# An attention and Fourier-mixing kernel on one core: x is kept on the chip between the two stages

## The chip, the cores and the metric

The kernel runs on one core of one Trainium2 chip. The metric is device microseconds of one execution, from the start of the program to its end. The engines of the core work from queues of their own, each in program order: TensorE (PE in the profile; PEld is its weight load), VectorE (DVE), ScalarE (ACT), GpSimd (POOL) and SyncE (SP), which in this kernel issues almost all DMAs.

## The reference

Two blocks follow each other. The first is an attention with random features (8 batches, 8 heads, 576 rows, head size 64, 128 features), the second a Fourier mixing with a residual, a layer norm and a two-layer MLP (512 to 2048 to 512):

```python
def phi(x):                       # x is q or k, scaled by 64 ** -0.25
    proj = np.einsum('bhsd,md->bhsm', x, omega)
    h = proj - np.sum(x * x, axis=-1, keepdims=True) / 2.0
    h = h - np.max(h, axis=-1, keepdims=True)
    return np.exp(h) / np.sqrt(m)
kv  = np.einsum('bhsm,bhsd->bhmd', k_p, v)
num = np.einsum('bhsm,bhmd->bhsd', q_p, kv)
den = np.einsum('bhsm,bhm->bhs', q_p, k_p.sum(2))[..., None] + 1e-06
x   = (num / den)                 # then laid out as (b, s, 8 * 64)

X = np.fft.fft(np.fft.fft(x, axis=1), axis=2)
u = x + np.real(X)
un = (u - mean(u)) / np.sqrt(var(u) + 1e-06)
out = u + np.maximum(un @ w_ch1, 0.0) @ w_ch2
```

The inputs w_ch1 and w_ch2 arrive in 64-bit form and are narrowed to 32 bits on the chip; all products are done in 32 bits.

## The kernel before

**Order.** The kernel's author writes each piece of work as a generator of steps (`Step`: engine, estimated microseconds, what it needs and makes, which buffers it takes and gives). `Listing.run` lays the streams out by a list schedule with these estimates, and the instructions are emitted in that order. On the chip each engine then goes through its own list strictly in order and waits where a semaphore isn't there yet. So a transfer that is slower than its estimate stalls the engine that stands at the waiting instruction, whatever else is ready.

**Early stage.** Up to about 677 us the streams run side by side: three streams of head pairs (`attn`, 32 pairs n, 4 per batch), the mixing of each batch (`mix`, `residual`), the MLP of the first four tiles of 128 rows (`plain`: hp is the first product, op the second), the narrowing of the weights (`weights`, `narrow`: raw, w) and the norms of the first block of 512 rows (`block_norms`).

**A pair.** k and q of two heads are loaded (kq, three buffers), v is loaded into a frame with ones beside it (vd, three buffers). PE transposes k and q (tps, left PSUM by ACT as kqT), multiplies by omega (pp), DVE takes the maximum (nmx), ACT the exponential (e). kvp is the sum over the rows of k-features times v, and it is the reader of vd. The q-features are transposed (tps, qeT) and ndp is numerator and denominator: 18 products of 64 columns. DVE divides (rden, xo). The 576 rows of a head sit on 64 partitions with 9 rows each, row s = 9 p + r, and the two heads of the pair on the two halves of the partitions.

**From attention to mixing.** The mixing needs for each row s also its partner 576 - s. In the kernel before, SP stores xo to a DRAM tensor xs (L501, two DMAs a pair), copies the upper half of the rows backward into xb, from DRAM to DRAM (L508, one a pair), and, once all four pairs of a batch are there, loads both into a tile x of 97 partitions and 3 + 3 slots of rows (L519 to L526, five DMAs a batch).

**The mixing.** DVE adds and subtracts partners (half, L538), folds the columns in the same way (half, fold, L540, L548, L556), PE multiplies by the tables over the rows (yp, L577, tables cs and sn) and over the columns (ab), and `residual` puts sums together on DVE and POOL (bmp, and x, which is now u). u goes to a DRAM tensor us; the partners' half goes to uh, and one backward copy from DRAM to DRAM (L664) brings it into us. The norm of a row tile loads u from us (u, L687), normalises it and transposes it on PE (tp, L702); the second load (ur) adds u to the MLP's output.

**Late stage.** From about 677 us PE does the MLP of the other 4096 rows, in blocks of 512, by a seven-product scheme (L919, L1010); the norms of the next block run beside it.

The program prints lines of kernel.py; these are the functions that the diff touches.

Of the kernel before, what the change touches and what calls it, by code (L numbers as in the profile page):

```python
# [25 lines left out]
NC3 = 3  # L26
CW = 96
CP = CW + 1

# [99 lines left out]
def _tables(S, DM):  # L129

    nk = S // 2 + 1
    t = CW * np.arange(NC3)[None, :] + np.arange(CP)[:, None]
    w = np.where((t == 0) | (t == S // 2), 0.5, 1.0)
    w[0, 1:] = 0.0
    turn = (t[:, :, None] * np.arange(nk)) % S
# [21 lines left out]
def kernel(  # L157
# [19 lines left out]
    NK = S // 2 + 1  # L177
# [10 lines left out]
    NV = 3  # L188
    NKQ = 3
    NE = 7  # L190
    NHALF = 2
# [12 lines left out]
    assert MF == 128 and D == 64 and R == 9 and NK == NC3 * CW + 1 and NPLAIN * TP + NTB * TB == B * S  # L204
# [20 lines left out]
        bank=6, mm=2, kq=NKQ, turned=NS, e=NE, e1=NS, kv=NS, xo=2, x=1, fold=1, half=NHALF,  # L225
# [8 lines left out]

    vds = [fix.tile([P, R, 2 * (D + 1)], F32, name=f"vd{i}") for i in range(NV)]
    for vd in vds:
        nc.gpsimd.memset(vd[:], 0.0)
        for i in range(2):
            nc.gpsimd.memset(vd[D * i : D * i + D, :, (D + 1) * i + D : (D + 1) * i + D + 1], 1.0)
# [21 lines left out]
    om = att.tile([128, 2, D], F32, name="om", tag="xo", bufs=2)  # L261
# [6 lines left out]
    nc.gpsimd.memset(om2[:], 0.0)  # L268

# [55 lines left out]
    xs = [dram.tile([S, DM], F32, name=f"xs{b}") for b in range(B)]  # L325
    xb = [dram.tile([S // 2, DM], F32, name=f"xb{b}") for b in range(B)]
    us = [dram.tile([S, DM], F32, name=f"us{b}") for b in range(B)]
    uh = [dram.tile([S // 2, DM], F32, name=f"uh{b}") for b in range(B)]
# [12 lines left out]
    def transposed(src, name, after, makes, give):  # L341

        dst = None
        for j0, j1 in ((0, 4), (4, 8), (8, 9)):
            m = j1 - j0
            yield Step(
                PE,
                0.11 * m,
                after=after(j0, j1),
                take=("bank",) + (("turned",) if j0 == 0 else ()),  # L350
                give=give(j0, j1),
            )
            if dst is None:
                dst = att.tile([128, R, 128], F32, name=name, tag="turned")
            ps = bank("tps")
            for j in range(j0, j1):
                nc.tensor.transpose(ps[:, (j - j0) * 128 : (j - j0 + 1) * 128], src(j), ident[:])  # L357
            yield Fork(evicted(dst, ps, j0, j1, makes))
        return dst

    def evicted(dst, ps, j0, j1, makes):
# [32 lines left out]
    def attn(n):  # L394
# [7 lines left out]
            "kqT",  # L402
            lambda j0, j1: (),
# [45 lines left out]
        def keep():  # L449
# [11 lines left out]
            "qeT",  # L461
            lambda j0, j1: tuple(("e", n, t) for t in range((R + j0) // 4, (R + j1 - 1) // 4 + 1)),
            ("qeT", n),
            lambda j0, j1: {4: ("e",), 8: ("e",), R: ("e1",)}[j1],
# [4 lines left out]
            after=(("kv", n), ("qeT", n, 0), ("qeT", n, 4), ("qeT", n, 8)),  # L469
# [4 lines left out]
        for r in range(R):  # L474
            for i in range(2):
                cols = slice(D * i, D * i + D)
                nc.tensor.matmul(
                    ndp[r // 5][cols, (D + 1) * (r % 5) : (D + 1) * (r % 5 + 1)],
                    lhsT=qeT[:, r, cols],
                    rhs=kvs[0][:, i, :],  # L480
                )
        yield Step(DVE, 1.6, take=("xo",), give=("bank", "bank"))
        xo = att.tile([P, R, D], F32, name="xo", tag="xo", bufs=2)
        rden = small.tile([P, R], F32, name="rden", tag="rden")
        parts = []
        for g, (r0, r1) in enumerate(((0, 5), (5, R))):
            nd = ndp[g][:, 0 : (D + 1) * (r1 - r0)].rearrange("p (r d) -> p r d", d=D + 1)
            nc.vector.tensor_scalar(rden[:, r0:r1], nd[:, :, D], DEN_EPS, None, op0=ALU.add)
            parts.append((r0, r1, nd))
        nc.vector.reciprocal(out=rden[:], in_=rden[:])  # L490
        for r0, r1, nd in parts:
            nc.vector.tensor_tensor(  # L492
                out=xo[:, r0:r1, :],
                in0=nd[:, :, 0:D],
                in1=rden[:, r0:r1].unsqueeze(2).to_broadcast([P, r1 - r0, D]),
                op=ALU.mult,
            )
        yield Step(SP, 1.3, 3.0, give=("xo",), makes=("xs", n))
        for i in range(2):
            h = 2 * pr + i  # L500
            nc.sync.dma_start(  # L501
                xs[b].rearrange("(p r) c -> p r c", r=R)[:, :, h * D : (h + 1) * D],
                xo[D * i : D * i + D],
            )

        yield Step(SP, 0.6, 4.0, after=(("xs", n),), makes=("x", b, pr))
        cols = slice(2 * pr * D, (2 * pr + 2) * D)
        nc.sync.dma_start(  # L508
            xb[b][:, cols].rearrange("t (i d) -> i t d", i=2),
            xs[b][S - 1 : S // 2 - 1 : -1, cols].rearrange("t (i d) -> i t d", i=2),  # L510
        )


    def mix(b):
        NR = 2 * NC3
        yield Step(SP, 2.4, 5.0, after=tuple(("x", b, pr) for pr in range(NP)), take=("x",))
        x = fft.tile([CP, NR, DM], F32, name="x", tag="x")
        lo, hi = x[:, 0:NC3, :], x[:, NC3:NR, :]
        nc.sync.dma_start(lo[0:CW], xs[b][0 : S // 2, :].rearrange("(c p) d -> p c d", p=CW))  # L519
        nc.sync.dma_start(lo[CW:CP], xs[b][CW : S // 2 + 1 : CW, :].unsqueeze(0))  # L520

        nc.sync.dma_start(
            hi[1:CP], xb[b].rearrange("(c p) d -> p c d", p=CW)
        )
        nc.sync.dma_start(hi[0:1, 0, :], xs[b][0:1, :])
        nc.sync.dma_start(hi[0:1, 1:NC3, :], xb[b][CW - 1 : 2 * CW : CW, :].unsqueeze(0))  # L526


        fold, mid_t = None, None

        def folds(n, **more):
            op = (ALU.add, ALU.subtract)[n]
            even, odd = (ALU.subtract, ALU.add) if n else (ALU.add, ALU.subtract)
            yield Step(NONE, **more)
            h = fft.tile([CP, NC3, DM], F32, name="half", tag="half", bufs=NHALF)
            for c in range(NC3):
                yield Step(DVE, 0.64, port=True)
                nc.vector.tensor_tensor(out=h[:, c], in0=lo[:, c], in1=hi[:, c], op=op)  # L538
                yield Step(DVE, 0.37, port=True)
                nc.vector.tensor_tensor(  # L540
                    out=h[:, c, 1 : 2 * QD],
                    in0=h[:, c, 1 : 2 * QD],
                    in1=h[:, c, DM - 1 : 2 * QD : -1],
                    op=op,
                )
                yield Step(DVE, 0.48, port=True)
                for m, o in ((0, even), (1, odd)):
                    nc.vector.tensor_tensor(  # L548
                        out=fold[:, c, 2 * n + m, :],
                        in0=h[:, c, 0:QD],  # L550
                        in1=h[:, c, 2 * QD : QD : -1],
                        op=o,
# [557 lines left out]
```

## Time and profile before

| what | value |
|---|---|
| median of 3 runs | 1477.3 us (1474.4, 1477.3, 1478.4) |
| the profiled execution's own time | 1469.33 us |
| its span, first to last instruction | 1467.6 us |
| mean granted TensorE clock | 0.948 |
| PE busy over the span | 1323.8 us (90%) |
| DVE, ACT, POOL busy | 574.7, 408.3, 304.7 us (39%, 28%, 21%) |
| DMA | 139573 packets, 113.56 MB; 99058 packets under 512 B |

Busy time counts instructions that compute. A wait is idle time of an engine right before an instruction, with what released it: in `PE yp L577 <- DVE xo L492` PE stood before the product yp until DVE had come past an instruction of line 492, because both the divide and the folding stand in the one list of DVE. Rows of SP's queue (SPq) give the time that issuing one or more DMAs took, not how long the data was under way.

### The profile page before, as it was taken

Reading aid. Unit: us, or ns where it says so; the run is one execution under the profiler, and the core shown is the slowest. Engines: PE = TensorE matmul, PEld = TensorE weight load, DVE = VectorE, ACT = ScalarE, POOL = GpSimd, SP = SyncE. Lnnn points to the kernel's source line nnn. Section 1 sums busy time; section 2 is a strip of 40 time slices with the busy share of each in tenths; the row PEclk is TensorE's granted clock in tenths of the full one; section 3 lists DMA queues with packets and bytes.
Section 4 is the critical chain, followed back from the end, with each engine's and each line's share of the span. In section 5 each row is a group of like instructions: output and inputs, shape, how many; then the busy total and the mean of one; then the engine's idle time right before and its main releaser. Section 6 shows DMA issues by size and latency. Waiting matters only on the chain.

```text
span 1467.6 us, 20379 instructions
## 1 busy us (share of the span) xinstructions
PE 1323.8 (90%) x7777; PEld 1146.4 (78%) x7777; DVE 574.7 (39%) x1412; ACT 408.3 (28%) x1199; POOL 304.7 (21%) x421
## 2 busy tenths in 40 slices
PE   6959396796989898688999999999999999999999
PEld 5848285675977787475888888888888888888887
DVE  3847474575654555344521412312213123122111
ACT  5836163543535444121202102011021021120110
POOL 1303032220100010111503304214033042140330
PEclk9979698898999899889999999999999999999999
DMA  8737364753534643312001010020010100200100
GB/s 217 203 96 191 86 170 122 198 149 98 139 94 120 170 101 94 95 50 72 3 20 65 15 56 17 15 72 1 22 65 15 43 30 15 72 1 15 58 1 29
DMA packets 139573, 113.56 MB, mean 77 GB/s; under 512 B 99058, under 2 KB 103906, under 8 KB 139476
## 3 DMA queue, kind: packets, MB, share of 16 engines
q1 hardware_dynamic: 134868, 95.48, 23.4%
q0 software_dynamic: 4608, 16.78, 3.7%
q8 instruction: 62, 1.02, 0.3%
q14 instruction: 35, 0.29, 0.1%
HBM read 83.92 MB, written 37.73 MB: 83 GB/s over the span
## 4 chain that ended last, share of the span: by engine, by line
PE 77%; DMA 11%; SPq 5%; DVE 4%; issue 2%; POOL 0%; ACT 0%; DVEq 0%; POOLq 0%
PE sx L1010 15%; PE sx L919 15%; PE sz L919 8%; PE sz L1010 8%; PE pp L418 5%; PE yp L577 4%; PE sy L919 4%; PE sy L1010 4%; PE kvp L440 3%; PE hp L764 3%; PE tps L357 3%; SPq L519 2%; DMA u<-us 2%; DMA xs<-xo 2%; PE op L787 2%
## 5 line engine op out<-in xcount | busy, mean ns | idle before, releaser
L386 ACT ACTIVATE e<-pp,nmx 128x128 f32<-128x128 f32 x576 | 157.3, 395 | 107.8 <-DVE nmx L374 107.6
L418 PE MATMUL pp<-om,kqT 128*128 128x256 f32 x576 | 145.9, 403 | 0.7 <-ACT qeT L363 0.6
L983 POOL TENSOR_TENSOR hs<-ht,ht 128x256 f32<-128x256 f32 x64 | 48.5, 758 | 469.2 <-DVE ht L906 469.2
L933 ACT ACTIVATE s<-sx 128x256 f32<-128x256 f32 x128 | 48.9, 383 | 347.7 <-PE sx L919 326.7
L919 PE MATMUL sx<-unT,w 128*128 128x256 f32 x512 | 131.2, 380 | 0.9 <-DVE ur L801 0.9
L374 DVE TENSOR_REDUCE nmx<-pp 128x4 f32<-128x512 f32 (+1 forms) x160 | 96.4, 632 | 79.8 <-PE pp L418 72.2
L418 PEld LDWEIGHTS pp<-om,kqT 128*128 128x128 f32 x576 | 112.2, 203 | 18.2 <-ACT qeT L363 1.0
L1010 PE MATMUL sx<-w,ht 128*128 128x256 f32 x512 | 114.4, 379 | 0.0
L919 PEld LDWEIGHTS sx<-unT,w 128*128 128x128 f32 x512 | 97.3, 190 | 14.8 <-issue 1.7
L1010 PEld LDWEIGHTS sx<-w,ht 128*128 128x128 f32 x512 | 96.8, 190 | 12.7
L906 DVE CUSTOM_DVE_ANT_0 ht<-sz,s 128x256 f32<-128x256 f32 x64 | 27.1, 425 | 185.1 <-PE sz L919 185.1
L1021 DVE TENSOR_TENSOR ur<-ur,sx 128x256 f32<-128x256 f32 x64 | 27.0, 422 | 140.0 <-PE sx L1010 140.0
L440 PEld LDWEIGHTS kvp<-vd,e 128*128 128x128 f32 x576 | 74.0, 196 | 4.9 <-issue 1.2
L440 PE MATMUL kvp<-vd,e 128*128 128x130 f32 x576 | 75.7, 282 | 0.5 <-ACT e L386 0.4
L304 POOL TENSOR_TENSOR w<-w,raw 128x512 f32<-128x512 f32 x32 | 45.7, 1437 | 144.7 <-DVE raw L302 142.3
L919 PE MATMUL sz<-tt,w1s 128*128 128x256 f32 x256 | 67.3, 387 | 5.7 <-DVE w1s L891 5.7
L966 ACT ACTIVATE ht<-sx 128x256 f32<-128x256 f32 x64 | 24.5, 383 | 171.0 <-PE sx L919 171.0
L637 POOL TENSOR_TENSOR x<-x,bmp 97x257 f32<-97x257 f32 x24 | 18.8, 782 | 254.6 <-DVE bmp L629 254.3
L702 PE MATMUL tp<-ident,u 128*128 128x128 f32 x144 | 23.3, 290 | 53.3 <-DVE u L698 48.6
L357 PE MATMUL tps<-ident,kq 128*128 128x128 f32 x288 | 48.0, 304 | 24.6 <-DMA kq<-in_k_dram 20.7
L577 PE MATMUL yp<-cs_sb,fold 97*128 97x289 f32 x96 | 34.4, 520 | 39.5 <-DVE xo L492 23.8
L764 PE MATMUL hp<-unT,w 128*128 128x128 f32 x512 | 67.6, 287 | 1.1 <-ACT unT L706 0.7
(102 smaller groups left out, 2395.7 us busy)
## 6 DMA issues: line engine op xcount, KB each, us to landing
raw<-in_moe_w_ch_dram POOLq DMA_DIRECT2D x32, 512.0 KB, 6.6
kq<-in_k_dram SPq DMA_DIRECT2D x32, 288.0 KB
kq<-in_q_dram SPq DMA_DIRECT2D x32, 288.0 KB
vd<-in_v_dram SPq DMA_DIRECT2D x64, 144.0 KB
xs<-xo SPq DMA_DIRECT2D x64, 144.0 KB
out_dram<-ur SPq DMA_DIRECT2D x36, 256.0 KB
u<-us SPq DMA_DIRECT2D x32, 256.0 KB
ur<-us SPq DMA_DIRECT2D x32, 256.0 KB
```

Of the source, the lines that this page charges most:

```text
L304: nc.gpsimd.tensor_tensor(out=dst, in0=dst, in1=lof, op=ALU.add)
L357: nc.tensor.transpose(ps[:, (j - j0) * 128 : (j - j0 + 1) * 128], src(j), ident[:])
L374: nc.vector.tensor_reduce(nmx[:, 0:num], ps[:, 0 : MF * num].rearrange("p (c m) -> p c m", m=MF), axis=AX.X, op=ALU.max, negate=True,)
L386: nc.scalar.activation(out=e[:, c, :], in_=ps[:, MF * c : MF * c + MF], func=AF.Exp, bias=nmx[:, c : c + 1],)
L418: nc.tensor.matmul(ps[:, 256 * j : 256 * j + 256], lhsT=kqT[:, 2 * t + j, :], rhs=om2[:].rearrange("p i m -> p (i m)"),)
L440: nc.tensor.matmul(kvp[:, 0 : 2 * (D + 1)], lhsT=feature(r), rhs=vds[n % NV][:, r, :], start=(r == 0), stop=(r == R - 1),)
L577: nc.tensor.matmul(yp[:, 0:NK], lhsT=fold[:, c, n, :], rhs=tab[:, c, :], start=(c == 0), stop=(c == NC3 - 1),)
L764: nc.tensor.matmul(hp[:, 0:TP], lhsT=w1[:, dc, 128 * fc : 128 * fc + 128], rhs=unTs[key][:, dc, :], start=(dc == 0), stop=(dc == NDC - 1),)
L919: nc.tensor.matmul(ps[:, 0:HT], lhsT=left(dc), rhs=right(dc), start=start and dc == 0, stop=(dc == D2 - 1), skip_group_check=True,)
L933: nc.scalar.activation(out=s[:], in_=ps[:, 0:HT], func=AF.Copy)
L983: nc.gpsimd.tensor_tensor(out=o, in0=l, in1=r, op=op)
L1010: nc.tensor.matmul(ps[:, 0:HM], lhsT=left(fc), rhs=right(fc), start=start and fc == 0, stop=(fc == HF - 1), skip_group_check=True,)
```

## The change

The rows of the attention are put in PSUM where the mixing needs them, so that x never leaves the chip.

- **Layout.** Row s = 9 p + r has its partner at 9 (63 - p) + (9 - r): the partner of slot r is slot 9 - r with the partitions reversed. When ACT takes the transposed q-features of the slots 5 to 8 out of PSUM, it reads the partitions backward. The 18 products of ndp then write slot r = 1 to 4 and its partner 9 - r to the same partitions (`SLOTS`); one PSUM bank is one head. The mixing has 128 partitions and two slots for partners, plus slot 0, whose rows are each other's partners, on 64 partitions.
- **x.** Two fixed tiles, for even and odd batches, are written by DVE's divide, now twelve instructions a pair where it was five, and read by the folds. A pair may write into its tile when the batch two before has been stored (`frames`). The store to xs, the copy to xb and the load of x are gone.
- **Buffers.** The frames for v are two, not three; the buffer for xo is gone; half and y, which shared two buffers, have one each.
- **Folding.** Partners are added for two slots in one instruction (128 x 1024), and so on; 7 instructions for each of the two signs where it was 13.
- **Tables.** cs and sn are 128 x 3 x 320 instead of 97 x 3 x 289, and yp has 320 columns. The third slot of ab has 64 rows.
- **u.** us has rows in the order of the slots. uh holds two slots instead of three; the backward copy moves 512 KB in four column blocks of 512 B where it moved 574 KB in two of 1 KB. The tiles of 128 rows are now pairs of slots of one batch (slot 0: of two batches), written to the output by two DMAs of rows with stride 9 instead of one. The first four tiles are the slots 1 to 4 of the batches 0 and 1; they need no backward copy.

The diff, without the parts that only rename sizes:

```diff
+SLOTS = {1: (0, 0), 2: (1, 0), 3: (0, 1), 4: (1, 1), 8: (0, 2), 7: (1, 2), 6: (0, 3), 5: (1, 3)}
+SLOTS[0] = (0, 4)
...
-    NV = 3
+    NV = 2
...
-        bank=6, mm=2, kq=NKQ, turned=NS, e=NE, e1=NS, kv=NS, xo=2, x=1, fold=1, half=NHALF,
+        bank=6, mm=2, kq=NKQ, turned=NS, e=NE, e1=NS, kv=NS, x0=1, x1=1, fold=1, half=1, y=1,
...
+        ps = ps[:, 0 : 128 * (j1 - j0)].rearrange("q (c p) -> q c p", p=128)
         nc.scalar.activation(
-            out=dst[:, j0:j1, :].rearrange("q c p -> q (c p)"),
-            in_=ps[:, 0 : 128 * (j1 - j0)],
-            func=AF.Copy,
+            out=dst[:, j0:j1, :], in_=ps[:, :, ::-1] if back else ps, func=AF.Copy
         )
...
-        for r in range(R):
-            for i in range(2):
-                cols = slice(D * i, D * i + D)
+        for i, order in enumerate(((0, 2, 1, 4, 3, 7, 8, 5, 6), (2, 1, 4, 3, 7, 8, 5, 6, 0))):
+            for r in order:
+                g, slot = SLOTS[r]
+                c0 = D * (1 - i if r >= 5 else i)
                 nc.tensor.matmul(
-                    ndp[r // 5][cols, (D + 1) * (r % 5) : (D + 1) * (r % 5 + 1)],
-                    lhsT=qeT[:, r, cols],
+                    ndp[i][D * g : D * g + D, (D + 1) * slot : (D + 1) * slot + D + 1],
+                    lhsT=qeT[:, r, c0 : c0 + D],
                     rhs=kvs[0][:, i, :],
                 )
...
-        yield Step(SP, 1.3, 3.0, give=("xo",), makes=("xs", n))
+        yield Step(DVE, 2.0, after=(("frame", b),), give=("bank", "bank"), makes=("x", b, pr))
+        x = xts[b % 2]
+        rden = small.tile([P, 2, 5], F32, name="rden", tag="rden")
         for i in range(2):
-            nc.sync.dma_start(
-                xs[b].rearrange("(p r) c -> p r c", r=R)[:, :, h * D : (h + 1) * D],
-                xo[D * i : D * i + D],
-            )
-        yield Step(SP, 0.6, 4.0, after=(("xs", n),), makes=("x", b, pr))
-        nc.sync.dma_start(
-            xb[b][:, cols].rearrange("t (i d) -> i t d", i=2),
-            xs[b][S - 1 : S // 2 - 1 : -1, cols].rearrange("t (i d) -> i t d", i=2),
-        )
+            nd = ndp[i][:, 0 : 5 * (D + 1)].rearrange("p (c d) -> p c d", d=D + 1)
+            cols = slice((2 * pr + i) * D, (2 * pr + i + 1) * D)
+            for p1, c0, c1 in ((P, 0, 4), (64, 4, 5)):
+                den = rden[0:p1, i, c0:c1]
+                nc.vector.tensor_scalar(den, nd[0:p1, c0:c1, D], DEN_EPS, None, op0=ALU.add)
+                nc.vector.reciprocal(out=den, in_=den)
+                nc.vector.tensor_tensor(
+                    out=x[0:p1, c0:c1, cols], in0=nd[0:p1, c0:c1, 0:D], in1=..., op=ALU.mult,
+                )
+    def frames():
+        for b in range(B):
+            yield Step(NONE, take=(f"x{b % 2}",), makes=("frame", b))
...
-        yield Step(SP, 2.4, 5.0, after=tuple(("x", b, pr) for pr in range(NP)), take=("x",))
-        x = fft.tile([CP, NR, DM], F32, name="x", tag="x")
-        nc.sync.dma_start(lo[0:CW], xs[b][0 : S // 2, :].rearrange("(c p) d -> p c d", p=CW))
-        ...
+        yield Step(NONE, after=tuple(("x", b, pr) for pr in range(NP)), take=("fold",))
+        x = xts[b % 2]
...
+            nc.vector.tensor_tensor(out=h[:, 0:NL], in0=x[:, 0:NL], in1=x[:, NL : 2 * NL], op=op)
...
             nc.sync.dma_start(
-                us[b][S // 2 + 1 : S, :].rearrange("t (i d) -> i t d", i=2),
-                uh[b][S // 2 - 1 : 0 : -1, :].rearrange("t (i d) -> i t d", i=2),
+                us[b][nh : 2 * nh, :].rearrange("t (i d) -> i t d", i=4),
+                uh[b][nh - 1 :: -1, :].rearrange("t (i d) -> i t d", i=4),
             )
...
+    tiles = [(b, n) for b in range(2) for n in (1, 3)] + [(b, n) for b in range(2) for n in (5, 7)]
...
-        nc.sync.dma_start(outf[128 * t : 128 * t + 128, :], ur[:])
+        store_rows(t, ur)     # for h, _, rows, _ in rows_of(t): nc.sync.dma_start(rows, src[h])
```

How the lists of two engines read at the places that the prediction speaks of. The first is SP's list around the backward copy of a batch: batch 3 before (the row at L664; L519 to L526 load x of batch 4), batch 2 of the changed kernel (the row at L660; vd and kq are loads of pairs).

```order
L644 DMA us_135<-x 96x512
L508 DMA xb_128<-xs_120 2x288x64
L647 DMA uh_143<-x 96x512
L664 DMA us_135<-uh_143 2x287x256
L519 DMA x<-xs_120 96x3x512
L520 DMA x<-xs_120 1x3x512
L522 DMA x<-xb_128 96x3x512
L525 DMA x<-xs_120 1x512
L526 DMA x<-xb_128 1x2x512
L501 DMA xs_121<-xo 576x1x64 x2
L508 DMA xb_129<-xs_121 2x288x64
```

```order
L640 DMA uh_127<-x_109 128x512 x2
L643 DMA us_119<-x_109 128x512 x2
L643 DMA us_119<-x_109 64x512
L660 DMA us_119<-uh_127 4x256x128
L254 DMA vd_101<-in_v_dram 64x9x64 x2
L248 DMA kq<-in_k_dram 128x576
L251 DMA kq<-in_q_dram 128x576
L254 DMA vd_102<-in_v_dram 64x9x64 x2
```

Behind the backward copy stood the load of x, and later stores and copies of the next pair; now a load of v stands there. Of the eight copies, six have a load of v as the next load behind them, and a seventh a load of u and then one of v.

The second place is PE's list before the mixing of batch 3 (yp), with the pairs around it; vd_91 to vd_93 before and vd_101, vd_102 in the changed kernel are the frames of v, and `x18` of ndp is one pair.

```order
L418 MATMUL pp<-om_111,kqT 128x256 x4
L477 MATMUL ndp<-kv,qeT 64x65 x18
L418 MATMUL pp<-om_111,kqT 128x256 x5
L440 MATMUL kvp<-vd_93,e 128x130 x8
L787 MATMUL op<-w_64,ht 128x512 x2
L764 MATMUL hp<-unT,w_63 128x128 x4
L577 MATMUL yp<-cs_sb,fold 128x289 x6
```

```order
L451 MATMUL kvp<-vd_101,e 128x130 x9
L368 MATMUL tps<-ident,e 128x128 x9
L493 MATMUL ndp<-kv,qeT 64x65 x18
L803 MATMUL op<-w_64,ht 128x512 x2
L451 MATMUL kvp<-vd_101,e 128x130 x9
L368 MATMUL tps<-ident,e 128x128 x9
L368 MATMUL tps<-ident,kq 128x128 x17
L429 MATMUL pp<-om_99,kqT 128x256 x2
L572 MATMUL yp<-cs_sb,fold 128x320 x6
L429 MATMUL pp<-om_99,kqT 128x256 x2
L572 MATMUL yp<-sn_sb,fold 128x320 x6
```

The last ndp of the batch now stands right ahead of the mixing that needs it. Two kvp that read the same frame follow each other with three groups between them; before, the three frames took turns. In the whole list of the changed kernel, 20 of the 32 kvp follow another that read the same frame.

More of the change, by code (lines that the diff above doesn't have):

```diff
@@ L535, in folds @@
[L535 to L539, printed above, removed]
+            yield Step(DVE, 1.25, take=("half",), port=True)
+            h = fft.tile([P, NC3, DM], F32, name="half", tag="half")
+            nc.vector.tensor_tensor(out=h[:, 0:NL], in0=x[:, 0:NL], in1=x[:, NL : 2 * NL], op=op)
@@ L544, in folds @@
                     op=op,
                 )
[L546 to L552, printed above, removed]
-                    )
-            yield Step(DVE, 0.2, makes=("fold", b, n), give=("half",), port=True)
+            yield Step(DVE, 1.2, makes=("fold", b, n), give=("half",), port=True)
@@ L560, in mix @@
-        mid_t = small.tile([CP, NC3, 1], F32, name="mid", tag="mid", bufs=2)
-        yield from folds(0, take=("half",))
-        yield Fork(folds(1, take=("half",)))
+        yield from folds(0)
+        yield Fork(folds(1))
         y = None
@@ L849 @@
     listing.run(
[L850 removed]
+        [first(), loads(), frames(), plain_norms(), mixing()]
         + [pairs(i) for i in range(NS)]
```

212 lines of the change are left out of this document (108 added, 104 removed).

## Prediction

> **What bounds the kernel now.** I read four views in this order: busy time by stage, PE's waits, PE's timeline at the long waits, and SP's queue at the same places. First the stages (columns: stretch, its length, busy time of PE, PEld, DVE, ACT, POOL with instruction counts, granted clock, DMA share, GB/s):
>
> ```profile
> 0.00:677.00 677.00, 537.79 (x4089) 454.07 (x4089) 365.72 (x936) 293.61 (x915) 107.68 (x137) 0.89 0.49 131
> 677.00:1468.00 791.00, 786.00 (x3688) 692.33 (x3688) 208.95 (x476) 114.73 (x284) 197.05 (x284) 1.00 0.09 31
> 500.00:600.00 100.00, 92.45 (x753) 80.67 (x753) 55.24 (x158) 45.82 (x146) 7.76 (x11) 0.95 0.37 95
> ```
>
> From 677 us on PE is busy 786 of 791 us at clock 1.00: the late stage is bound by PE, and the change adds nothing to PE there. The early stage is not: PE is idle 677.0 - 537.8 = 139.2 us, and its clock is 0.89. DVE, at 366 of 677 us, is not the bound either. So the answer lies in those 139 us. Whom PE waited for in the early stage, in total, times, longest:
>
> ```profile
> PE tp L702 <- DVE u L698: 48.6, 3, 24.3
> PE yp L577 <- DVE xo L492: 23.8, 3, 11.6
> PE tps L357 <- DMA kq<-in_k_dram: 20.7, 7, 6.7
> PE yp L577 <- ACT e L386: 15.6, 1, 15.6
> PE op L787 <- POOL w L304: 6.8, 2, 6.1
> PE sz L919 <- DVE w1s L891: 5.7, 1, 5.7
> PE omps L335 <- POOL ident masks.py:199: 5.6, 1, 5.6
> PE tp L702 <- ACT e L386: 4.7, 1, 4.7
> PE tps L357 <- DMA kq<-in_q_dram: 2.6, 5, 1.4
> ```
>
> These nine are 134.1 of the 139.2 us. The names of the releasers mislead: yp needs the folds, and DVE does them late. SP's queue and two rows of PE and DVE show why, at the end of batch 3 and of batch 6:
>
> ```profile
> 332.63 0.61 SPq L508 DMA_DIRECT2D xb<-xs  x1
> 333.35 3.23 SPq L647 DMA_DIRECT2D uh<-x  x1
> 339.13 0.60 SPq L664 DMA_DIRECT2D us<-uh  x1
> 339.82 8.44 SPq L519 DMA_DIRECT2D x<-xs  x1
> 349.36 0.40 SPq L522 DMA_DIRECT2D x<-xb  x1
> ...
> 362.90 5.33 PE L577 MATMUL yp<-cs_sb,fold 97*128 97x289 f32 x12 [11.59 <-DVE xo L492]
> ...
> 601.74 1.21 SPq L501 DMA_DIRECT2D xs<-xo  x2
> 605.14 0.64 SPq L508 DMA_DIRECT2D xb<-xs  x1
> 607.30 2.11 SPq L664 DMA_DIRECT2D us<-uh  x1
> 609.64 8.30 SPq L687 DMA_DIRECT2D u<-us  x1
> ...
> 624.69 0.69 DVE L692 BATCH_NORM_STATS2 st<-u 128x6 f32<-128x512 f32 x1 [11.30 <-DMA u<-us]
> ```
>
> A backward copy holds up the DMA that is issued behind it: 339.13 to 348.26, so 9.1 us, behind L664 (574 KB), and 332.63 to 336.58, so 4.0 us, behind L508 (144 KB). At 339.82 it is the load of x that is held up, and PE stands 11.6 us at yp; at 609.64 it is a load of u, and with it DVE and PE's tp stand. The change takes away the load of x and all 32 copies L508, and leaves the eight copies L664.
>
> **The change, part by part.**
>
> *A. The load of x.* PE's waits at yp are 23.8 + 15.6 = 39.4 us. They end with the load, but yp now waits for DVE, from the last ndp on: divide and first fold. The prices of DVE:
>
> ```profile
> L492 DVE TENSOR_TENSOR xo<-ndp,rden 128x320 f32<-128x320 f32 x32 | 15.7, 491 | 9.0 <-DMA xs<-xo 7.9
> L492 DVE TENSOR_TENSOR xo<-ndp,rden 128x256 f32<-128x256 f32 x32 | 13.3, 414 | 0.0
> L490 DVE RECIPROCAL rden<-rden 128x9 f32<-128x9 f32 x32 | 6.9, 216 | 1.1
> L488 DVE TENSOR_SCALAR rden<-ndp 128x4 f32<-128x4 f32 x32 | 5.1, 159 | 4.5 <-PE ndp L477 4.5
> L538 DVE TENSOR_TENSOR half<-x 97x512 f32<-97x512 f32 x48 | 32.8, 684 | 44.6 <-DMA x<-xs 30.2 <-DMA x<-xb 14.4
> L540 DVE TENSOR_TENSOR half<-half 97x255 f32<-97x255 f32 x48 | 20.4, 425 | 1.7
> L548 DVE TENSOR_TENSOR fold<-half 97x128 f32<-97x128 f32 x96 | 23.7, 289 | 1.6
> L556 DVE COPY mid<-half 97x3 f32<-97x3 f32 x8 | 1.3, 163 | 0.0
> ```
>
> A divide is now twelve instructions: 4 x 0.16 to add, 4 x 0.20 to invert (a little under L490), 2 x 0.41 for 256 elements and 2 x 0.18 for 64 (0.077 us per 64 from the two L492 rows), so 2.6 us where it was 2 x 0.16 + 0.22 + 0.49 + 0.41 = 1.4. One sign of the folds is 1.20 us (1024 elements, at the 1.0 ns per element between L538 and L540) + 0.16 + 0.68 + 0.43 + 2 x 0.55 + 0.16 = 3.7, so 7.5 a batch where it was 79.6 / 8 = 9.95. From the last ndp to yp DVE needs 2.6 + 3.7 = 6.3 us. At batch 3 PE has op, kvp, 26 tps and two pp between the two, by these rows and the kvp row below 1.7 + 2.0 + 2.8 + 0.9 = 7.4 us; elsewhere 4.5 to 10 us.
>
> ```profile
> 597.48 1.72 PE op L787 x4
> 42.26 3.88 PE pp L418 x18
> 46.15 2.01 PE kvp L440 x18
> 290.89 1.97 PE tps L357 x18
> 599.20 1.22 PE ndp L477 x36
> ```
>
> (The trace has two records for each product, one for each transpose.) So I leave 1 us of waiting a batch: 8 us. A = -31, between -39 and 0.
>
> *B. The loads of u.* tp waits 48.6 + 4.7 = 53.3 us. The first four tiles need no backward copy now, and stores and copies L501, L508 no longer stand ahead of them. But a u load still waits behind the stores of u, and the last one in the list stands behind those of batch 7; from the end of batch 7's products to that load's tp pass three residuals, a store, the load and the norm, beside twelve op (10.3 us at 0.86). I leave a quarter, 13 us. B = -40, between -53 and 0.
>
> *C. v in two frames.* The third frame was its cover: no wait for vd stands among PE's waits, and the same frame came back after three pairs. Now 20 kvp follow one that read the same frame. The reload starts when that kvp is done: issue 1.2 us and landing 2.2 us, from L501 above (the same 2 x 144 KB in 256 B pieces; 602.95 to 605.14, when L508 had waited for it). PE's work between the two is, by the rows above, 3.1 to 17.6 us, mean 6.8; in the list shown it is tps, ndp and op: 1.0 + 1.2 + 1.7 = 3.9. So without a hold-up these waits are near nothing; I take 3 us for all. Seven reloads stand behind a backward copy. The new copy moves 512 KB in 1024 pieces; by the L664 row's bytes it holds the queue 9.1 x 512 / 574 = 8.1 us, at least the 4.0 of L508, at most 9.1. With the copy issued 3 us ahead of the kvp (I cannot see this; SP is mostly idle, 0 to 8 is possible), the reload lands 8.1 - 3 + 0.6 + 2.2 = 7.9 us after it, less the 5.3 us of PE's work at these seven: 2.6 x 7 = 18. kq is queued behind v, so it is late with it; its waits outside the start, 20.7 + 2.6 - 6.7 = 16.6 us, had the queue's hold-ups as cause and mostly go; I keep 5. C = 3 + 18 + 5 - 16.6 = +9, between -17 and +60 (all seven at 11 us and 2 us on the rest).
>
> The Trainium skill ("DMA: Bandwidth & Descriptors", the section on why a DMA increments its semaphore by 16) says that a DMA is split over as many engines, at most 16, as divide both sides' slowest dimension. By that rule the old copy, whose slowest dimension is 2, ran on two engines and the new one, with 4, on four; the DMA share of 0.49 beside a held-up queue does not speak against it. That four engines halve the hold no trace here shows. It would then be about half, an estimate of 4 to 5 us by that page, and the 18 us in C nearly nothing: the sum would be some 17 us lower with the clock's part.
>
> *D. PE's own work.* yp has 320 columns for 289:
>
> ```profile
> L577 PE MATMUL yp<-sn_sb,fold 97*128 97x289 f32 x96 | 25.0, 407 | 0.5 <-ACT y L587 0.5
> ```
>
> 96 records in 25.0 us are 0.26 each; 31 / 289 more on 192 of them is +5. The number of the other products stays.
>
> *E. The clock.* Where PE waits less the clock is higher: 0.95 in 500 to 600 us with 92% busy, 0.89 on the whole. With 62 us of waits gone I expect 0.94: 537.8 x (1 - 0.89 / 0.94) = -29, between 0 and 537.8 x 0.11 = -59.
>
> *F. DVE and the rest.* DVE gets 32 x 1.17 - 8 x 2.5 = +18 us, on 366 of about 600: cover is there, I take +4 for moments when it isn't. ACT reads PSUM backward and POOL adds two slots instead of three: both far from the bound, 0. Tables are 0.3 MB larger in the start, where DMA is full: +1. The output goes in twice as many stores, one more issue of 0.6 us at the end: +1.
>
> Sum: -31 - 40 + 9 + 5 - 29 + 4 + 2 = -80. The profiled execution's 1469.3 us becomes 1389; the median of the runs stood 8.0 us above it, so 1397.
>
> **The rivals.**
>
> *Everything goes.* Only the start's waits (5.6 + 6.7), w (6.8) and the change of stage (5.7) stay, 25 us, and the clock is 0.98: -114 - 49 + 5 = -158, to 1319. For it: every other wait traces back to the queue. Against: lists made from estimates never fit quite. I count what ends under 1360 as this case: 0.2.
>
> *The copy L664 was the cause.* It stays, and behind it something else is late, u or v for x; L508 was hidden. Then only yp's 39 us and a third of the clock's gain go: -39 + 5 - 10, to about 1433. For it: the worst waits all stand behind L664. 0.2 for 1425 to 1465.
>
> *v is the new wait, and the kernel is slower.* Two frames under three streams make kvp wait. Each us of PE's waiting costs with the clock 29 / 62 more, 1.47; the gain is used up when each of the 20 reloads costs 80 / (20 x 1.47) = 2.7 us beyond my 1. If SP stands at a wait, its list holds v and every kq back: at 5 us a reload, 4 more than I took, +118, to 1515. Against: 6.8 us of PE's work against 3.4. 0.08.
>
> *No change to measure.* The waits only move to DVE, divide and fold being on the way now: 0.03. About 0.3%, 4 us, is what a measurement of this kernel can tell from no change.
>
> **How the numbers follow.** My forecast (1360 to 1425) has 0.49; everything goes 0.2, copy 0.2, slower 0.08, same 0.03. The range leaves out the lower part of "everything goes", the upper end of "copy", same and slower, 0.2 together: 1340 to 1455. Faster is 0.49 + 0.2 + 0.2 = 0.89.
>
> **What would show it.** Right: no PE wait at yp above 3 us; DMA share of the early stage about 0.4; the late stage starting near 595 us and as long as before; waits of kvp for vd in the list, 10 to 30 us; clock 0.93 or more in the early stage; the DMA behind L660 held 4 to 9 us. Wrong: kvp or tps waiting for vd or kq by more than 60 us; tp waiting as long as before; or a late stage that has changed.

## The result, and the profile after

The changed kernel takes 1387.2 us (median of 4 runs, 1384.1 to 1388.1) where the kernel before, on the same chip, takes 1476.3 us (1474.4 to 1478.4): ratio 0.939, 95% interval 0.937 to 0.941. The profiled execution of the changed kernel took 1387.4 us, 82 us less than that of before, and this time it stands at the median; the profiled execution of before had stood some 7 us below its own.

First the stages of the kernel after (same columns as before: stretch, length, busy PE, PEld, DVE, ACT, POOL, clock, DMA share, GB/s):

```profile
0.00:594.00 594.00, 532.66 (x4089) 447.32 (x4089) 377.40 (x1069) 294.44 (x910) 94.94 (x120) 0.97 0.39 109
594.00:1386.00 792.00, 784.62 (x3688) 690.21 (x3688) 209.34 (x476) 114.66 (x284) 196.91 (x284) 1.00 0.11 31
```

The late stage starts 83 us earlier and is as long as before (792 us for 791). In the early stage PE stands idle 594.0 - 532.7 = 61.3 us where it stood 139.2; its busy time fell by 5.1 us only, although the clock went from 0.89 to 0.97. The gain is waiting: 77.9 us of 83. Whom PE still waited for (total, times, longest):

```profile
PE tps L368 <- DMA kq<-in_k_dram: 27.0, 8, 8.6
PE kvp L451 <- DMA vd<-in_v_dram: 9.4, 4, 5.2
PE tp L719 <- DVE u L715: 5.7, 1, 5.7
PE omps L345 <- DMA om<-in_omega_dram: 3.1, 1, 3.1
...
PE sz L934 <- DVE w1s L906: 1.9, 1, 1.9
PE tps L368 <- DMA kq<-in_q_dram: 1.8, 4, 0.9
...
PE yp L572 <- DVE fold L547: 1.3, 1, 1.3
```

The two big entries of before are nearly gone: yp 1.3 us with this releaser for 39.4, tp 7.3 (5.7 and two of 0.8) for 53.3. New is kvp's wait for v, and the waits for k and q did not go. SP's queue in the kernel after, around the backward copies L660 of two batches:

```profile
249.72 0.64 SPq L660 DMA_DIRECT2D us<-uh  x1
259.15 1.24 SPq L254 DMA_DIRECT2D vd<-in_v_dram  x2
260.44 0.62 SPq L248 DMA_DIRECT2D kq<-in_k_dram  x1
...
267.79 1.36 SPq L254 DMA_DIRECT2D vd<-in_v_dram  x2
269.19 1.56 SPq L248 DMA_DIRECT2D kq<-in_k_dram  x1
...
554.50 0.65 SPq L660 DMA_DIRECT2D us<-uh  x1
556.62 3.31 SPq L689 DMA_DIRECT2D ur<-us  x1
```

After seven of the eight copies SP's next DMA comes only 7 to 34 us later (here 249.72 to 259.15), so the copy holds up nobody: the loads of v that follow it in the list go out later than its hold lasts. Only the last has one right behind it: the load of ur is through at 559.93, 5.4 us after the copy's issue began. And at 267.79 a load of v is issued late, because its frame is still read, and k of a pair stands right behind it in the one queue; PE's timeline shows who pays:

```profile
265.51 2.25 PE L451 MATMUL kvp<-vd,e 128*128 128x130 f32 x18 [1.46 <-DMA vd<-in_v_dram]
...
273.11 0.63 PE L368 MATMUL tps<-ident,kq 128*128 128x128 f32 x4 [4.36 <-DMA kq<-in_k_dram]
```

### The profile page after: what moved, and what is told of

Read it like the earlier page. It is cut to its first block, busy times and chain, and to the rows that moved or that the text cites. A ratio compares the mean times of both kernels' runs of the same rounds, so it can differ in the third digit from the quotient of the medians.

```text
span 1385.7 us, 20262 instructions
## 1 busy us (share of the span) xinstructions
PE 1317.3 (95%) x7777; PEld 1137.5 (82%) x7777; DVE 586.7 (42%) x1545; ACT 409.1 (30%) x1194; POOL 291.8 (21%) x404
## 4 chain that ended last, share of the span: by engine, by line
PE 85%; DMA 6%; DVE 4%; SPq 2%; issue 1%; ACT 1%; POOL 1%; DVEq 0%; ACTq 0%; POOLq 0%
PE sx L1024 16%; PE sx L934 16%; PE sz L1024 8%; PE sz L934 8%; PE pp L429 7%; PE sy L1024 4%; PE hp L780 4%; PE sy L934 4%; PE yp L572 4%; PE op L803 4%; PE tps L368 3%; PE kvp L451 3%; PE ndp L493 2%; DMA kq<-in_q_dram 2%; PE ab L599 2%; DMA kq<-in_k_dram 2%
## 5 line engine op out<-in xcount | busy, mean ns | idle before, releaser
L429 PE MATMUL pp<-om,kqT 128*128 128x256 f32 x576 | 140.7, 391 | 1.1 <-ACT kqT L375 1.1
L429 PEld LDWEIGHTS pp<-om,kqT 128*128 128x128 f32 x576 | 108.7, 196 | 20.5 <-issue 2.0
L368 PEld LDWEIGHTS tps<-ident,kq 128*128 128x128 f32 x288 | 37.3, 157 | 40.8 <-issue 28.8
L375 ACT ACTIVATE kqT<-tps 128x512 f32<-128x512 f32 (+1 forms) x96 | 43.7, 497 | 82.1 <-PE tps L368 81.8
L934 PE MATMUL sx<-tt,w 128*128 128x256 f32 x256 | 65.6, 379 | 1.0 <-DVE ht L921 1.0
L934 PE MATMUL sz<-unT,w1s 128*128 128x256 f32 x256 | 65.5, 379 | 0.0
```

Source lines behind the costliest of these rows:

```text
L429: nc.tensor.matmul(ps[:, 256 * j : 256 * j + 256], lhsT=kqT[:, 2 * t + j, :], rhs=om2[:].rearrange("p i m -> p (i m)"),)
L934: nc.tensor.matmul(ps[:, 0:HT], lhsT=left(dc), rhs=right(dc), start=start and dc == 0, stop=(dc == D2 - 1), skip_group_check=True,)
```

## The experiments

All times are medians; the ratio is to the kernel before, measured beside each kernel. "Order unchanged" means that every engine's list is that of the kernel it starts from, but for the edit itself.

| kernel | us | ratio, 95% interval |
|---|---|---|
| before, L664 in four blocks | 1434.6 | 0.971 (0.968 to 0.974) |
| before, L664 on POOL's queue | 1448.9 | 0.981 (0.979 to 0.983) |
| before, L664 and L508 in four blocks | 1420.6 | 0.962 (0.960 to 0.963) |
| before, two frames for v | 1482.4 | 1.004 (1.003 to 1.006) |
| after | 1387.2 | 0.939 (0.937 to 0.941) |
| after, L660 in two blocks | 1390.8 | 0.941 (0.938 to 0.945) |
| after, stores and copies of x put back, no reader | 1441.6 | 0.976 (0.972 to 0.980) |
| after, only the stores put back | 1388.1 | 0.940 (0.938 to 0.942) |
| after, more work in the divide | 1445.0 | 0.978 (0.976 to 0.980) |
| after, less work in the divide | 1383.1 | 0.938 (0.935 to 0.941) |
| after, k and q ahead of v | 1361.2 | 0.922 (0.920 to 0.925) |
| after, third frame for v | 1370.8 | 0.929 (0.927 to 0.931) |
| after, k and q ahead, less work in the divide | 1353.1 | 0.918 (0.915 to 0.921) |

**The old copy in four blocks.**

```
-  us[...].rearrange("t (i d) -> i t d", i=2), uh[...].rearrange("t (i d) -> i t d", i=2)
+  us[...].rearrange("t (i d) -> i t d", i=4), uh[...].rearrange("t (i d) -> i t d", i=4)
```

> The kernel before, with the backward copy L664 cut into four blocks of columns instead of two, all else and the order unchanged. Theory 1 (what paid in the change is the round trip of x as a whole: store, copy L508, load): a shorter hold behind L664 gives back some 3 to 4 us at the few places where something stands behind it, 5 to 15 us in all, 1462 to 1472 us; yp's waits stay above 25 us. Rival (the copy L664 in two blocks was the cause): the waits at yp and tp, 39 and 53 us, at least halve, 40 us or more are gone, under 1437 us. Both: the DMA behind L664 waits about 5 us instead of 9.

It took 1434.6 us, 41 us less than before (34 between the two profiled executions): the rival's number, and far outside theory 1's. SP's queue at batch 3, the place shown in the prediction, and then PE's waits of this kernel:

```profile
331.77 0.65 SPq L664 DMA_DIRECT2D us<-uh  x1
332.51 5.26 SPq L519 DMA_DIRECT2D x<-xs  x1
```

```profile
PE tp L702 <- DVE u L698: 40.4, 3, 19.1
PE yp L577 <- ACT e L386: 19.6, 1, 19.6
PE yp L577 <- DVE xo L492: 12.0, 3, 7.9
PE tp L702 <- ACT e L386: 4.6, 1, 4.6
PE yp L577 <- DVE nmx L374: 1.4, 1, 1.4
```

The hold is 331.77 to 337.77, 6.0 us for 9.1. While almost nothing but the copy is under way, the DMA share is 0.29 (334 to 337 us) where it was 0.14 before (342 to 348 us): some four and two of the 16 engines. But yp's and tp's waits did not halve: 78.0 us for 92.7. The rest of the gain is spread: PE's wait for the weights (op, 6.8 us) is gone, that at the change of stage fell from 5.7 to 1.1, and PE's busy time in the early stage is 6 us less. So cutting this copy into four blocks gives about half of what the whole change gains, though not by the places alone that I had named. Why the weights also came in time isn't settled.

**The old copy on another queue.**

```
-  nc.sync.dma_start(us[b][S // 2 + 1 : S, :]...
+  nc.gpsimd.dma_start(us[b][S // 2 + 1 : S, :]...
```

> The kernel before, with the backward copy L664 issued on POOL's queue instead of SP's, all else and the order unchanged. Theory 1 (the round trip of x): the hold behind L664 is gone from SP's queue, but x still waits for the last pair's store, its copy L508 and five loads: 10 to 30 us gone, 1447 to 1467 us, and yp still waits over 15 us. Rival (the copy L664 was the cause): 50 us or more gone, under 1427 us, yp's and tp's waits under 25 us together.

1448.9 us, 27 us less, inside theory 1. The hold is gone from SP's queue, yet yp waits 23.3 us and tp 26.5:

```profile
PE tp L702 <- DVE u L698: 26.5, 3, 10.3
PE yp L577 <- ACT e L386: 17.8, 1, 17.8
PE hp L764 <- ACT ht L750: 8.3, 1, 8.3
PE yp L577 <- DVE xo L492: 5.5, 2, 3.5
```

The waits at hp are not among the longer ones of before. So without any hold by L664 the load of x still kept yp waiting, and the waits for the weights (6.8 us) and at the change of stage (5.3) stayed. Moving the copy is no substitute for shortening it.

**Both old copies in four blocks.** As the first edit, and the same for L508.

> The kernel before, with both backward copies, L664 and L508, in four blocks of columns instead of two, order unchanged. L664 alone in four blocks gave 1434.6 us. Theory (the hold behind every backward copy is on the path, not that of L664 alone): the hold behind L508 falls from 4.0 to about 2.7 us and the time by 8 us or more, under 1427 us. Rival (L508 lies beside other work, only L664 counts): within 5 us of 1434.6. A loss is possible if pieces of 128 B cost more than the two more engines save: over 1440 us.

1420.6 us: another 14 us, so L508's hold, 4.0 us in 32 places, was on the path too. In one place it fell to 3.3 us (257.52 to 260.86), where 2.7 had been expected.

**The new copy in two blocks.** The first edit the other way, i=4 to i=2, in the kernel after.

> The kernel after, with the backward copy L660 cut into two blocks of columns instead of four, order unchanged. Theory 1: only one DMA in the whole list stands right behind L660 (a load of ur, 5.4 us after it, and tp behind that): that one is held some 8 to 9 us, and the time goes up 0 to 5 us (1387 to 1392 us). Rival (four blocks instead of two are what made the copy harmless): 3 us or more at each of the eight copies, +15 us or more, over 1402 us.

1390.8 us, 3.6 us more than the kernel after, with intervals that overlap: theory 1. The one place:

```profile
557.27 0.64 SPq L660 DMA_DIRECT2D us<-uh  x1
559.27 6.18 SPq L689 DMA_DIRECT2D ur<-us  x1
```

8.2 us, 557.27 to 565.45, for 5.4 in four blocks. The same step that gave 41 us in the kernel before is worth next to nothing here, because there is hardly a DMA right behind the copy any more.

**The removed traffic put back, without a reader.**

```
+  nc.sync.dma_start(xs[b]...[:, :, h * D : (h + 1) * D], x[:, :, h * D : (h + 1) * D])   # two a pair
+  nc.sync.dma_start(xb[b][:, cols].rearrange("t (i d) -> i t d", i=2), xs[b][S - 1 : S // 2 - 1 : -1, cols]...)
```

> The kernel after, with the removed traffic put back without a reader: after each divide two stores of its columns of x into memory and a backward copy of 288 rows in two blocks, on SP's queue, and nothing reads them; the load of x stays away; the order of all else is unchanged. Theory 1a (the stores and copies cost by holding up SP's queue): loads of k, q and v come late, their waits grow from 38 us to 60 us or more, 1405 to 1440 us. Theory 1b (only the chain through the load of x cost anything, the rest was hidden): within 5 us of the kernel after, 1382 to 1394 us.

1441.6 us, 54 us more, just above the range of 1a (1405 to 1440); 1b has fallen. PE's waits in this kernel, and SP's queue at one of the places:

```profile
PE kvp L453 <- DMA vd<-in_v_dram: 48.6, 8, 14.9
PE tps L370 <- DMA kq<-in_k_dram: 26.5, 9, 8.0
```

```profile
58.46 4.47 SPq L524 DMA_DIRECT2D xs<-x  x2
65.02 0.61 SPq L529 DMA_DIRECT2D xb<-xs  x1
65.72 4.53 SPq L254 DMA_DIRECT2D vd<-in_v_dram  x2
```

The copy can go out only when the two stores have landed (62.93 to 65.02, SP stands), and then the load of v behind it is through only at 70.25. PE's kvp waits 8.0 us for that load.

**Only the stores put back.** The same edit without its second line.

> The kernel after, with only the two stores of x after each divide put back (no reader, no backward copy), order of all else unchanged. With stores and copies it was 1441.6 us, 54 above the kernel after. Theory (a copy in two blocks holds the queue, a store doesn't): most of the 54 us is the copies', 1387 to 1405 us here, waits of kvp for v under 20 us. Rival (the stores' issue time and their small pieces cost as much as the copies): half of it or more stays, 1414 us or more.

1388.1 us, no difference to the kernel after. Sixty-four stores of 160 KB on SP's queue cost nothing that can be measured; the whole 54 us is the copy, with its wait for the stores. Those two parts, the hold and the wait, weren't separated.

**Two frames in the kernel before.** `NV = 3` becomes `NV = 2`.

> The kernel before, with two frames for v instead of three and all else as it was (the planner makes its list anew). Theory (my term C: a reload behind a held queue comes late): kvp waits for v 20 to 50 us in all, 1490 to 1530 us. Rival (PE's work between two uses of a frame covers the reload, and only the planner's order changes): kvp waits under 10 us, 1465 to 1485 us.

1482.4 us, about 5 us more. kvp's wait for v:

```profile
PE kvp L440 <- DMA vd<-in_v_dram: 15.8, 5, 5.7
```

So the waits come, somewhat under the 21 us that term C took for v and under the theory's 20; the time is within the rival's range. The planner's list is another one (yp waits longer, tp less), so 5 us is not the frame's price alone.

**A third frame in the kernel after.** `NV = 2` becomes 3, and one buffer less for bmp.

> The kernel after, with a third frame for v, the room for which comes from one buffer less for the residual's tile bmp (the planner makes its list anew). Theory (the two frames make v late and, behind it in SP's queue, k and q): kvp's waits go (9.4 us), kq's fall to 15 or less, 1365 to 1380 us. Rival (the waits for k and q have another cause, or the missing bmp buffer gives the gain back): 1383 us or more.

1370.8 us, 16.4 us less than the kernel after, in the theory's range. The waits of kvp for v are down to 0.9 us. What then leads the list:

```profile
PE tps L368 <- DMA kq<-in_k_dram: 18.1, 5, 9.1
PE yp L572 <- DVE fold L547: 9.7, 3, 5.4
PE tps L368 <- DMA kq<-in_q_dram: 6.2, 4, 5.2
```

24.3 us of 28.8 stay, more than the 15 expected, and yp waits 8 us more; the planner's list is another one, so the pieces can't be added up.

**k and q ahead of v.**

```
   yield Step(SP, 0.45, 4.0, makes=("kq", n))          # k and q of pair n
   ...
-  yield Step(SP, 1.3, 4.5, take=(f"vd{n % NV}",), makes=("vd", n))     # v of pair n
   ...
+  if n: yield from v_load(n - 1)                                       # v of the pair before
```

> The kernel after, with the load of each pair's v put behind the next pair's loads of k and q in the list of loads instead of ahead of them (the planner makes its list anew). Theory (k and q wait in SP's queue behind a load of v that waits for its frame): tps' waits for kq fall from 28.8 us to under 15 (8.6 of them the start), 1370 to 1382 us. Rival (v is then the late one: kvp's waits for v grow by as much): 1384 us or more, kvp's waits over 20 us.

1361.2 us, 26 us less than the kernel after, more than the theory said:

```profile
PE kvp L457 <- DMA vd<-in_v_dram: 9.8, 4, 5.2
PE tps L374 <- DMA kq<-in_q_dram: 4.3, 5, 2.9
PE tps L374 <- DMA kq<-in_k_dram: 3.5, 4, 1.1
```

The waits for k and q fell from 28.8 to 7.8 us, and v is no later than it was (9.8 for 9.4). The wait of 8.6 us at the start is among those gone, its place in the list being another one now; the other 12 us are, as far as a kernel with a new list can show it, what k and q lost behind a load that waits for its frame.

**More work in the divide.**

```
-  for p1, c0, c1 in ((P, 0, 4), (64, 4, 5)):
+  for p1, c0, c1 in ((P, 0, 4), (64, 4, 5), (64, 4, 5), (64, 4, 5)):
```

> The kernel after, with the small part of every divide (64 rows, 64 elements for each of two heads: add, invert, multiply) done three times over instead of once: 12 more instructions a pair at 0.14 to 0.22 us each, 32 x 2.0 = 66 us of DVE work, the result the same and the order unchanged. Theory (DVE has cover all but at the end of a batch, where the divide stands ahead of the folds and yp waits): +2 us at each of eight batches at most, 1388 to 1404 us. Rival (DVE's latency counts at each pair, since PSUM's banks come free only after the divide): 32 us or more, over 1419 us.

1445.0 us, 58 us more, for 62 us of DVE's busy time: the rival's number, and no cover at all. The early stage of this kernel (its profiled execution took 1451 us):

```profile
0.00:653.00 653.00, 557.50 (x4079) 460.27 (x4080) 439.04 (x1452) 294.71 (x910) 95.23 (x120) 0.93 0.35 99
```

DVE is busy 67% of it. PE's idle time grew from 61 to 95.5 us in many short waits (before pp 11.7 us for 1.1, before ndp 5.1 for 0.5, before yp 9.2 for 2.1), and its busy time by 25 us. Most of that is the clock's: it stands at 0.50 in 15 stretches with 73.1 us of PE's busy time, where the kernel after has 8 with 30.2, and half of the difference, what half speed would cost, is 21 us. Yet only seven waits are longer than 3.4 us, for six. Short waits bring it down as well; two stretches that follow each other (length, busy PE, clock, DMA share, GB/s; the longest wait around them is 1.35 us):

```profile
225.17:228.58 3.41, 1.62 (x7) 1.00 0.00 0
228.58:231.99 3.41, 3.20 (x11) 0.50 0.00 0
```

The rival's reason, that PSUM's banks come free only after the divide, wasn't tested by itself: a fuller DVE and a later end of each divide come together here.

**Less work in the divide.**

```
+  nc.tensor.matmul(ndp[i][D : 2 * D, (D + 1) * 4 : (D + 1) * 5], lhsT=qeT[:, 0, D * i : D * i + D], ...)
   ...
-  for p1, c0, c1 in ((P, 0, 4), (64, 4, 5)):
+  for p1, c0, c1 in ((P, 0, 5),):
```

> The kernel after, with six instructions of DVE for a divide instead of twelve: one more product for each head fills the other 64 rows of the fifth group (with a copy of row 0's result, which the tables' zero weights drop), so that all five groups are divided at once on 128 rows. By after's rows that takes 2 x (0.140 + 0.155 + 0.217) = 1.02 us from a divide and adds 2 x 0.08 for 64 more elements: 0.86 us less, 27 us of DVE in 32 pairs; PE gets 64 products of 0.04 us, 2.5 us. The order of all else is unchanged. Theory (DVE is on the path at most pairs; 66 us more of it cost 57 us, 0.87 for each): 27 x 0.87 - 2.5 = 21 us faster, about 1366 us. Rival (more DVE work hurts from some load on, less of it helps nobody, since after's PE waits name DVE for few us): within 5 us, 1383 to 1393 us.

1383.1 us, 4 us less than the kernel after, with intervals that overlap: the rival's range.

```profile
0.00:585.79 585.79, 530.98 (x4217) 448.15 (x4218) 355.56 (x879) 294.28 (x912) 94.95 (x120) 0.97 0.39 111
```

DVE did 22 us less. The profiled execution was 5 us below the median (1377.8 us), and in it the late stage starts 10 us earlier. DVE's price is not one number: little at 377 us of work, nearly one for one at 439.

**Both that helped.**

> The kernel after with both: k and q ahead of the earlier pair's v (alone 1361.2 us) and the divide in six instructions (alone 1383.1 us median, 1377.8 at its fastest, against 1387.2 for the kernel after). The order of all else is that of the kernel with k and q first. Theory (the lighter divide still shortens what stands ahead of PE now that PE waits less for loads): another 4 to 10 us, 1351 to 1357 us. Rival (DVE has cover again and the 64 added products cost 2.5 us): 1359 to 1365 us.

1353.1 us, 8 us below k and q first alone, inside the theory's range; the two intervals just touch (0.915 to 0.921 and 0.920 to 0.925). That the lighter divide helps here is likely, not certain: one of its five times, 1359.1, lies in the rival's range. It is 34 us faster than the kernel after and the fastest version here. What is left in PE's waits:

```profile
PE kvp L457 <- DMA vd<-in_v_dram: 7.7, 3, 5.3
PE tps L374 <- DMA kq<-in_k_dram: 4.2, 4, 1.9
```

## Why the prediction was right, and where it was not

The sum was right, -80 against -82 between the two profiled executions, and that is partly luck, because errors of both signs met. That the waits at yp and tp would go was right. But of the forecast -80 us, -56 were waits (A, B, C, F and the rest) and -24 PE's busy time (D and E); measured are -78, -5 and +1 for the late stage. Against the medians the gain is 89 us: the 8 us that I added for the profiled execution's place belonged to that one execution, and without them the forecast would have been 1389.

*A, the waits at yp.* -31 forecast; 39.4 became 1.3, and 0.4 more with another releaser: -37.7. The 8 us left to be waited for at the ends of batches didn't come. The sizes of DVE's steps were right, as after's rows show:

```profile
L508 DVE TENSOR_TENSOR x<-ndp,rden 128x256 f32<-128x256 f32 x64 | 27.2, 425 | 2.2
L508 DVE TENSOR_TENSOR x<-ndp,rden 64x64 f32<-64x64 f32 x64 | 13.9, 217 | 2.2
```

*B, the waits at tp.* -40 forecast; 53.3 became 7.3 (5.7 and two of 0.8): -46.0. The quarter that I left was too much.

*C, v and kq.* +9 forecast; kvp's 9.4 and, for k and q, 28.8 - 23.3 = 5.5 make +14.9. Two of its parts failed. The reloads of v do follow the copies in the list, but go out only when the hold is over, so the 18 us for seven held reloads never arose (the forecast had said that it couldn't see how far the copy is issued ahead). And the 16.6 us of k's and q's waits that were to go stayed: I took the copies as their cause, and the run with k and q ahead of v shows most of it to be the head of the queue, a load of v that waits for its frame; a third frame takes less of it away. Part of them never was the copies': in the kernel before, too, SP stood 43.9 us at loads of v until a frame was free (154.6 us in the kernel after), and two of its waits for k, 2.0 and 2.5 us, follow such stands (SP until 191.00 and 311.98, PE until 199.88 and 316.92). "kq is queued behind v, so it is late with it" stood in the working, at 5 us; it was some 20 outside the start.

The hold behind L660 was 5.4 us, between the 4.0 and 9.1 that I gave as bounds. By its bytes I had taken 8.1, which is what two blocks measure, 8.2. The rule of the Trainium skill ("DMA: Bandwidth & Descriptors", the section on why a DMA increments its semaphore by 16), by which four blocks run on four engines and two on two, has the right sign: 574 KB went from 9.1 to 6.0 us, 512 KB from 8.2 to 5.4. The DMA shares of 0.29 and 0.14 beside the old copy agree with four and two engines. Half was my estimate by that rule; measured are two thirds.

*D, yp wider.* +5 forecast. The products of the table sn, which no wait precedes, went from 25.0 to 27.3 us for half of yp, so +4.6 for the whole:

```profile
L572 PE MATMUL yp<-sn_sb,fold 128*128 128x320 f32 x96 | 27.3, 433 | 0.4 <-ACT y L582 0.4
```

*E, the clock.* -29 forecast, and this is the term that failed most: PE's busy time fell by 5.1 us, with D's 4.6 taken out by about 10. The step that was wrong is the multiplication of busy time by the ratio of two mean clocks. The mean clock of a stage is a mean over time, waits included. Two stretches of the kernel before, at the wait at yp of batch 3 and right behind it, show that the low clock lies where PE does little:

```profile
350.00:366.00 16.00, 4.42 (x16) 3.14 (x16) 8.67 (x26) 0.28 (x1) 0.00 (x0) 0.61 0.51 146
366.00:380.00 14.00, 13.63 (x102) 12.10 (x102) 10.80 (x35) 6.75 (x21) 3.18 (x5) 0.95 0.44 115
```

What a wait does cost is the products right behind it, which run slow. The twelve at 362.90, behind 11.6 us of waiting, took 5.33 us; the same twelve of another batch, with no wait ahead, in the kernel before:

```profile
182.04 3.09 PE L577 MATMUL yp<-cs_sb,fold 97*128 97x289 f32 x12
```

That wait cost 2.2 us on top. The clock stood at 0.50 until 367.30: 4.4 us at half speed and 0.9 at full speed make the 3.1. So the price is at most half of PE's busy time in the stretches at 0.50. These are 16 in the early stage of the kernel before and 8 in that of the kernel after; in sum (length, busy PE):

```profile
sum 150.20, PE 70.90; mean PE 4.43
sum 40.97, PE 30.19; mean PE 3.77
```

That is at most 35 us before and 15 after, 20 us less if all of that work ran at half speed. The clock was thus worth 10 to 20 us; the two bounds differ because other products changed too (ndp, in its new order, went from 41.4 to 45.1 us).

The Trainium skill ("TensorE: Matmul & The Clock Gate", Part 1: The HAM clock gate) says that after about 3.4 us of idling PE runs at half speed until it has been busy about as long. Thirteen waits of before's early stage are longer than that, six of after's; seven fewer at half of 3.4 us each would be 12 us, an estimate by that page, and it lies in the trace's range. Long waits are not all of it, as the run with more work in the divide shows.

*F, DVE.* +18 us of work forecast, +11.7 in the stage's rows (365.7 to 377.4); +4 us of time, and 22 us less work gave back 4, within the noise. So the work was put 6 us too high, and the +4 us weren't measured by themselves. "Cover is there" was not a safe reason: 62 us on top cost 58.

*Not forecast.* PE's waits for the weights (6.8 us), at the change of stage (5.7 to 1.9) and at the very start (5.6 to 3.1) shrank by 13 us. The first two also shrank when only the old copy was cut into four blocks, but stayed (6.8 and 5.3 us) when it was moved to POOL's queue, which also loads the weights; why is open.

So -38 - 46 + 15 - 13 = -82 for these waits, some 4 us given back in small ones, -5 of busy time, +1 for the late stage.

*The rivals.* "Everything goes" (1319) didn't come: k, q and v still wait. "The copy L664 was the cause" put 1433 on a change that leaves the copy, and the time was 1387; but the run that shortens that copy alone in the kernel before took 1434.6. What made that rival wrong for this change is that the new queue has hardly anything right behind the copy, whether in four blocks or in two. "v is the new wait" had the right place and too high a price: 20 reloads at 2.7 us would have used up the gain, and all of them together waited 9.4. Of the signs named ahead, yp under 3 us, DMA share 0.39, the late stage from 594 us, clock 0.97 and the hold of 5.4 us came; kvp's waits were just below the 10 to 30 named.

What the change pays for is shown by the runs in the main: stores of x are free, a copy behind them costs 54 us in the new kernel, and copies in four blocks give the old one 57 of the 89 us without keeping x on the chip at all. How the other 32 us divide between the load of x, the fewer foldings and the first tiles that need no copy, no run separates.

## What to carry to other kernels

On one in-order queue ask of each DMA two things: what stands right behind it while it holds the queue, and what it waits for itself while others stand behind it. A DRAM-to-DRAM copy on few blocks and a load that waits for a buffer are the two expensive heads; cut the first into more blocks, put the second behind the loads that could go. And price waits as waits: a stage's mean clock is low because of them, so busy time must not be scaled by it. What the clock costs is at most half of the busy time in the stretches at 0.50.

## What the runs showed of the hardware that was not expected

- A copy from DRAM to DRAM holds its queue by how it is cut: 574 KB 9.1 us in two blocks and 6.0 in four, 512 KB 8.2 and 5.4. In both cases four blocks take 0.66 of two. The hold ends before the copy does. By the DMA records of the four traces 238 of its 574 pieces of 1 KB, 450 of 1148 pieces of 512 B, 225 of 512 and 446 of 1024 had not begun at that moment: 110 to 120 for each block every time. So here the hold was the time in which all but these of a block's 256 or 287 pieces began.
- The clock falls to 0.50 without a long wait, too: behind 3.41 us in which PE was busy 1.62, with no wait above 1.35 us.
- The same cut is worth 41 us with a full queue behind it and at most a few us (3.6, within the intervals) with an empty one; 64 stores added to the same queue cost 0.9 us, within the noise.
- DVE's price in this program bends: 22 us less work gave 4 us, 62 us more cost 58 (in the early stage that was profiled, 34 of idle and 25 of busy time of PE), with DVE busy 64% of the early stage before that and 67% after.
